# Two heads of the first k load moved from the casting DMA queue to an uncast one, with the casts on VectorE and ScalarE

## The chip, the cores and the metric

The kernel runs on one core of a Trainium2 chip. The metric is the device time of one launch in microseconds, the median of several runs. A core has TensorE (PE in the profile; its weight loads are listed as PEld), VectorE (DVE), ScalarE (ACT), GpSimd (POOL) and SyncE (SP). Three engines issue DMAs here: SyncE, ScalarE and GpSimd, each through a queue of its own, and the transfers of all queues run on the core's 16 DMA engines. In this kernel only GpSimd's loads change the type (f32 in memory, f16 in the tile); the loads that SyncE and ScalarE issue keep it.

## The reference

An attention with projected keys and values (batch 8, 8 heads, 1024 positions, head size 64, projection to 64), followed by a two-way maxout layer (8192 tokens, 512 to 1024 to 512):

```python
k_proj = einsum('ks,bhsd->bhkd', E, k)          # E, F: 64 x 1024
v_proj = einsum('ks,bhsd->bhkd', F, v)
scores = (q @ k_proj.T) / sqrt(64)
attn = softmax(scores)                           # over the 64 projected keys
x = (attn @ v_proj) transposed to (8192, 512)
out = maximum(x @ w1, x @ w2) @ w_out            # f32, 8192 x 512
```

All inputs and the output are f32 in memory; inside, the kernel multiplies in f16 and accumulates in f32.

## The kernel before, in words

The order of all work is written out by hand: the program order of each engine is the order in which the Python code emits its instructions, and the framework only adds the waits. There are three parts. The start (to about 30 us) handles batch 0's attention and loads everything. Then come sixteen units, two for each batch, each an up product and a down product (L691, L783; both by a seven-product scheme with sums made on VectorE), with the attention of the next batch's groups woven in at named slots. At the end the last unit's results are stored.

The change lies in the start. In program order it does this:

- **E and F** (64 x 1024 f32 each, 256 KB) are loaded into `ef_sb`, E by SyncE's queue (L77) and F by ScalarE's queue (L78). ScalarE then loads its function table (L79).
- **GpSimd's queue** carries all casting loads, in this order: k heads 0 to 3 of batch 0 (then the identity matrix is made on GpSimd), q heads 0 to 3, k heads 4 to 7, q heads 4 to 7, four loads of two heads of v, fourteen pieces of w1 and w2, w_out (`wo_sb`, L133), and from L938 on batch 1's k, v, q and batch 2's k. A load of four heads is 512 KB in f16. GpSimd issues each load of the weights only when a load eight places earlier has landed.
- **TensorE** first runs eight filler matmuls on a tile of ones (`warm`, L143), then eight transposes of E (L157), two fillers, eight transposes of F (L157), two fillers, and then the projection of k heads 0 to 3 (`step_kv`, L185, eight matmuls). Then follow two fillers, transposes of the projected k (L275), two fillers, transposes of q (L301), scores (L330) and so on.
- **VectorE** fills the ones tile (L136), casts the identity (L149), and copies E's transposes out of PSUM into `eft[0]` (L164). **ScalarE** copies F's transposes into `eft[1]` (L164). The projection of k needs `eft[0]`, that of v `eft[1]`.

The tiles that the change touches: `tiles[0]["k"]` (f16, 128 partitions x 8 heads x 8 x 64; a partition holds eight consecutive positions of each head), and `wo_sb` (f16, 128 x 8 x 512, 8 KB in each partition), which is used only after it is loaded at L133, with its sums (L542) at about 39 us.

Of the kernel before, what the change touches and what calls it, by code (L numbers as in the profile page):

```python
# [8 lines left out]
FP32 = mybir.dt.float32  # L9
FP16 = mybir.dt.float16  # L10
# [6 lines left out]
def kernel(  # L17
# [12 lines left out]
    nc = tc.nc  # L30

    B, H, S, D = q.shape
    KP = E.shape[0]
    DM = moe_w1.shape[0]
    DF = moe_w1.shape[1]
    NC = S // 128
    NI = NC // 2
    NFB = DF // 128
# [6 lines left out]
    const = ctx.enter_context(tc.tile_pool(name="const", bufs=1))  # L45
# [27 lines left out]
    def big(n, dtype=FP16):  # L73
        return const.tile([128, 16384 // mybir.dt.size(dtype) // 2], dtype, tag=f"big{n}", name=f"big{n}")

    ef_sb = big(0, FP32)[0:KP, :].rearrange("k (i s) -> k i s", i=2)
    nc.sync.dma_start(out=ef_sb[:, 0, :], in_=E)  # L77
    nc.scalar.dma_start(out=ef_sb[:, 1, :], in_=F)  # L78
    nc.scalar.add_instruction(  # L79
        mybir.InstLoadActFuncSet(  # L80
            name=nc.get_next_instruction_name(),
# [15 lines left out]
    def load(t, n, src, b, h0, h1):  # L97
        nc.gpsimd.dma_start(
            out=t[n][:, h0:h1],
            in_=src[b, h0:h1].rearrange("h (p c) d -> p h c d", c=NC),  # L100
        )

    tiles = {b: {} for b in range(B)}
    for n in ("k", "q", "v"):
        alloc(tiles[0], n)
    for h0 in (0, H // 2):
        for n, src in (("k", k), ("q", q)):
            load(tiles[0], n, src, 0, h0, h0 + H // 2)
            if (h0, n) == (0, "k"):
                ident = const.tile([128, 128], FP32)  # L110
                make_identity(nc, ident)
# [2 lines left out]

    w1_sb = big(1).rearrange("p (r f) -> p r f", r=NDC)
    w2_sb = big(2).rearrange("p (r f) -> p r f", r=NDC)
    wo_sb = const.tile([128, NFB, DM], FP16)
    for g in range(2):
        for w_sb, w in ((w2_sb, moe_w2), (w1_sb, moe_w1)):
            nc.gpsimd.dma_start(  # L120
                out=w_sb.rearrange("p (g z) f -> p g z f", z=2)[:, g, :, 0:256],
                in_=w.rearrange("(g p z) f -> p g z f", p=128, z=2)[:, g, :, 0:256],
            )
    for w_sb, w, f0, f1 in (
# [3 lines left out]
        for z in range(2):  # L128
            nc.gpsimd.dma_start(
                out=w_sb.rearrange("p (g z) f -> p g z f", z=2)[:, :, z, f0:f1],  # L130
                in_=w.rearrange("(g p z) f -> p g z f", p=128, z=2)[:, :, z, f0:f1],
# [15 lines left out]
    warm(8)  # L147
    ident16 = const.tile([128, 128], FP16)
    nc.vector.tensor_copy(out=ident16, in_=ident)  # L149


    eft = [const.tile([128, NC, KP], FP16, tag=f"eft{i}", name=f"eft{i}") for i in range(2)]

    for i in range(2):
        eft_ps = mm_bank()
        for c in range(NC):
            nc.tensor.transpose(  # L157
                out=eft_ps[:, c * KP : (c + 1) * KP],
                in_=ef_sb[:, i].rearrange("k (p c) -> k c p", c=NC)[:, c, :],
# [890 lines left out]
    for b in range(3, B):  # L1050
        t = tiles[b]
        n = 2 * b - 3
# [13 lines left out]
    for i, (new, old) in enumerate(zip([*groups[1:], none], groups)):  # L1066
        n, h = divmod(i + 2, 2)
# [70 lines left out]
```

## Time and profile before

| | |
|---|---|
| time, median of 3 runs | 321.56 us (321.26 to 321.61) |
| profiled execution: span, first to last instruction | 320.8 us (its whole device time is not given by the page) |
| TensorE busy | 313.7 us, 98% of the span |
| VectorE, ScalarE, GpSimd busy | 75%, 64%, 13% |
| mean granted TensorE clock | 0.994 |
| GpSimd's queue | 28.31 MB, 56.3% of the 16 DMA engines' span |
| HBM | 57.15 MB read, 16.78 MB written |

How to read it: TensorE is busy nearly all the time, so the other engines' shares tell only how much room they have. The chain of work that ended last follows the last instruction back to what released each step; its pieces name an engine or a DMA and a line. An issue row names the engine whose queue issued a DMA (SPq, ACTq, POOLq), the size in KB as stored, and the time from the issue to the landing. In the rows by stretch of time, the columns are the length, the busy time and instruction count of PE, PEld, DVE, ACT and POOL, then the granted clock (1.00 is full speed), the mean busy share of the 16 DMA engines (above 1 where packets overlap) and the GB/s that they moved, counted as stored.

### The profile page before, as it was taken

Reading aid. Unit: us, or ns where it says so; the run is one execution under the profiler, and the core shown is the slowest. Engines: PE = TensorE matmul, PEld = TensorE weight load, DVE = VectorE, ACT = ScalarE, POOL = GpSimd, SP = SyncE. Lnnn points to the kernel's source line nnn. Section 1 sums busy time; section 2 is a strip of 40 time slices with the busy share of each in tenths; the row PEclk is TensorE's granted clock in tenths of the full one; section 3 lists DMA queues with packets and bytes.
Section 4 is the critical chain, followed back from the end, with each engine's and each line's share of the span. In section 5 each row is a group of like instructions: output and inputs, shape, how many; then the busy total and the mean of one; then the engine's idle time right before and its main releaser. Section 6 shows DMA issues by size and latency. Waiting matters only on the chain.

```text
span 320.8 us, 9165 instructions
## 1 busy us (share of the span) xinstructions
PE 313.7 (98%) x3918; PEld 253.3 (79%) x3918; DVE 239.5 (75%) x432; ACT 205.3 (64%) x371; POOL 40.6 (13%) x63
## 2 busy tenths in 40 slices
PE   8899999999999999999999999999999999999996
PEld 3464588788887888888887888788887888888885
DVE  1246789787969787796969696896969696969683
ACT  1186752777775777576776777477776777765541
POOL 8259102003000300012000400021000000000000
PEclk9799999999999999999999999999999999999999
DMA  7999999997988899899999999899979231303023
GB/s 134 204 200 187 199 206 202 207 193 120 204 155 149 168 194 245 220 190 165 222 228 200 169 203 244 204 169 159 227 153 218 53 101 35 100 33 101 33 101 130
DMA packets 76408, 53.14 MB, mean 166 GB/s; under 512 B 29520, under 2 KB 76240, under 8 KB 76368
## 3 DMA queue, kind: packets, MB, share of 16 engines
q0 software_dynamic: 30944, 28.31, 56.3%
q1 hardware_dynamic: 45056, 23.80, 31.3%
q8 instruction: 30, 0.49, 0.6%
q10 hardware_dynamic: 368, 0.46, 0.6%
q14 instruction: 10, 0.08, 0.1%
HBM read 57.15 MB, written 16.78 MB: 230 GB/s over the span
## 4 chain that ended last, share of the span: by engine, by line
PE 94%; DMA 3%; ACT 1%; DVE 1%; issue 0%; DVEq 0%; POOLq 0%
PE mm_ps L783 46%; PE mm_ps L691 27%; PE mm_ps L477 4%; PE mm_ps L185 4%; PE att_ps L342 3%; DMA k_sb<-in_k_dram 3%; PE mm_ps L330 2%; PE mm_ps L579 2%; PE att_ps L227 1%; PE mm_ps L143 1%; PE mm_ps L301 1%; ACT ex_sb L370 1%; PE att_ps L330 0%; DVE qt_sb L306 0%; ACT ld_sb L382 0%; PE att_ps L502 0%
## 5 line engine op out<-in xcount | busy, mean ns | idle before, releaser
L665 ACT COPY p_sb<-mm_ps 128x512 f32<-128x512 f32 x179 | 101.7, 592 | 49.4 <-PE mm_ps L691 27.3
L783 PEld LDWEIGHTS <-big 128*128 128x128 f16 x768 | 73.5, 98 | 11.8 <-issue 3.6
L783 PE MATMUL mm_ps<-T_sb,big 128*128 128x256 f16 x576 | 77.0, 273 | 0.0
L706 DVE TENSOR_TENSOR gt_sb<-mm_ps,p_sb 128x512 f16<-128x512 f32 x56 | 38.5, 688 | 43.4 <-PE mm_ps L691 43.0
L691 PE MATMUL mm_ps<-big,big 128*128 128x256 f16 x336 | 50.4, 273 | 0.0
L691 PEld LDWEIGHTS <-big 128*128 128x128 f16 x448 | 43.8, 98 | 5.1
L783 PE MATMUL mm_ps<-wo_sb,gt_sb 128*128 128x256 f16 x256 | 42.8, 273 | 0.0
L783 PEld LDWEIGHTS <-gt_sb 128*128 128x128 f16 x376 | 35.6, 98 | 7.0 <-issue 3.0
L423 ACT ACTIVATE ex_sb<-mm_ps 128x512 f16<-128x512 f32 x50 | 27.2, 596 | 18.1 <-PE mm_ps L330 12.8
L691 PEld LDWEIGHTS <-wd_sb 128*128 128x128 f16 x336 | 32.8, 98 | 4.1
L691 PE MATMUL mm_ps<-xt_sb,wd_sb 128*128 128x256 f16 x224 | 33.0, 272 | 0.0
L452 DVE TENSOR_TENSOR xt_sb<-att_ps,ld_sb 128x1024 f16<-128x1024 f32 x26 | 31.7, 1219 | 0.2
L783 PE MATMUL mm_ps<-m_sb,xt_sb 128*128 128x256 f16 x128 | 24.4, 273 | 0.0
L813 DVE TENSOR_TENSOR o_sb<-mm_ps,p_sb 128x512 f32<-128x512 f32 x32 | 21.9, 683 | 2.8 <-ACT p_sb L837 2.0
L293 POOL COPY junk<-qt_sb 1x1 f16<-1x1 f16 x6 | 1.5, 244 | 175.7 <-DMA qt_sb<-q_sb 175.7
L709 DVE TENSOR_SCALAR gt_sb<-gt_sb 128x512 f16<-128x512 f16 (+1 forms) x60 | 21.7, 362 | 2.1
L651 DVE TENSOR_TENSOR big<-gt_sb 128x1024 f16<-128x1024 f16 x32 | 21.8, 683 | 0.0
L783 PE MATMUL mm_ps<-wo_sb,big 128*128 128x256 f16 x128 | 21.5, 273 | 0.0
L752 ACT ACTIVATE gt_sb<-mm_ps 128x512 f16<-128x512 f32 x28 | 16.8, 601 | 5.7 <-PE mm_ps L691 5.7
L783 PE MATMUL mm_ps<-T_sb,gt_sb 128*128 128x256 f16 x120 | 20.3, 273 | 0.0
L783 PEld LDWEIGHTS <-xt_sb 128*128 128x128 f16 x188 | 18.4, 98 | 2.1
L706 DVE TENSOR_TENSOR gt_sb<-p_sb 128x512 f16<-128x512 f32 x28 | 19.1, 682 | 0.7 <-ACT p_sb L665 0.6
(110 smaller groups left out, 435.1 us busy)
## 6 DMA issues: line engine op xcount, KB each, us to landing
out_dram<-o_sb SPq DMA_DIRECT2D x62, 256.0 KB, 2.9
k_sb<-in_k_dram POOLq DMA_DIRECT2D x7, 1024.0 KB, 10.2
v_sb<-in_v_dram POOLq DMA_DIRECT2D x7, 1024.0 KB, 16.8
q_sb<-in_q_dram POOLq DMA_DIRECT2D x5, 1024.0 KB, 23.4
q_sb<-in_q_dram POOLq DMA_DIRECT2D x6, 512.0 KB, 14.8
big<-in_moe_w_dram POOLq DMA_DIRECT2D x12, 128.0 KB, 6.6
k_sb<-in_k_dram POOLq DMA_DIRECT2D x2, 512.0 KB, 9.5
v_sb<-in_v_dram POOLq DMA_DIRECT2D x4, 256.0 KB, 14.3
```

The source lines that it names most:

```text
L185: nc.tensor.matmul(out=kv_ps[r * KP : (r + 1) * KP, h * D : (h + nh) * D], lhsT=eft[i][:, c, :], rhs=t[w][:, h0 + h : h0 + h + nh, c, :], ...
L423: nc.scalar.activation(out=t["ex", g, j][:, e, :], in_=banks[e], func=ACTF.Exp, scale=scale)
L452: nc.vector.tensor_tensor(out=x_out(t, g, j).rearrange("q z o n -> q o z n"), in0=at_ps.rearrange("q o (z n) -> q o z n", z=2), in1=ld[:, ...
L477: nc.tensor.matmul(out=h_ps, lhsT=wd_sb[:, r, fb * 128 : (fb + 1) * 128], rhs=t["xt"][:, r, :, j * W : (j + 1) * W], start=(r == 0), stop= ...
L651: nc.vector.tensor_tensor(out=S(i), in0=S(0) if x is None else x, in1=y(), op=op)
L665: copy(out=x, in_=bank)
L691: nc.tensor.matmul(out=bank[:, m * W : (m + 1) * W], lhsT=w_[:, n_, (2 * d + m) * 128 : (2 * d + m + 1) * 128], rhs=a[:, n_, :], start=(n ...
L706: nc.vector.tensor_tensor(out=c_blk(j, c), in0=two(x), in1=two(y), op=ALU.add)
L709: nc.vector.tensor_scalar_max(ap, ap, 0.0)
L752: nc.scalar.activation(out=out, in_=in_, func=ACTF.Relu)
L783: nc.tensor.matmul(out=bank[i][:, 0:CH] if two_banks else bank[:, i * CH : (i + 1) * CH], lhsT=a(c)[:, i * 128 : (i + 1) * 128], rhs=w_(c) ...
L813: nc.vector.tensor_tensor(out=o_sb, in0=two(x), in1=two(y), op=ALU.add)
```

## The change

Heads 0 and 1 of batch 0's k are no longer part of the first casting load. SyncE's queue fetches them as f32 (512 KB) into a new view `kf_sb`, which lies in the memory that `wo_sb` takes later (both tiles have the tag `wo`). VectorE casts head 0 and ScalarE casts head 1 from there into the f16 tile; each cast stands behind the identity's cast in the emitted order, so on VectorE ahead of the copy into `eft[0]`, and on ScalarE ahead of the copy into `eft[1]`. GpSimd's first load now brings heads 2 and 3 only (256 KB in f16). E goes from SyncE's queue to ScalarE's, and F from ScalarE's to SyncE's, behind k. The first projection matmul of k now waits for GpSimd's load, for both casts and for `eft[0]`. The load of w_out now waits for the casts as well, as they read its memory. The order of instructions on TensorE is the same; VectorE and ScalarE have one instruction more each, SyncE one more DMA.

```diff
     ef_sb = big(0, FP32)[0:KP, :].rearrange("k (i s) -> k i s", i=2)
-    nc.sync.dma_start(out=ef_sb[:, 0, :], in_=E)
-    nc.scalar.dma_start(out=ef_sb[:, 1, :], in_=F)
+    kf_sb = const.tile([128, 2048], FP32, tag="wo", name="kf_sb")[:, 0 : 2 * NC * D].rearrange(
+        "p (h c d) -> p h c d", h=2, d=D
+    )
+    nc.scalar.dma_start(out=ef_sb[:, 0, :], in_=E)
+    nc.sync.dma_start(out=kf_sb, in_=k[0, 0:2].rearrange("h (p c) d -> p h c d", c=NC))
+    nc.sync.dma_start(out=ef_sb[:, 1, :], in_=F)
...
     for h0 in (0, H // 2):
         for n, src in (("k", k), ("q", q)):
-            load(tiles[0], n, src, 0, h0, h0 + H // 2)
+            load(tiles[0], n, src, 0, h0 + 2 * ((h0, n) == (0, "k")), h0 + H // 2)
...
-    wo_sb = const.tile([128, NFB, DM], FP16)
+    wo_sb = const.tile([128, NFB, DM], FP16, tag="wo", name="wo_sb")
...
     ident16 = const.tile([128, 128], FP16)
     nc.vector.tensor_copy(out=ident16, in_=ident)
+    nc.vector.tensor_copy(out=tiles[0]["k"][:, 0], in_=kf_sb[:, 0])
+    nc.scalar.copy(out=tiles[0]["k"][:, 1], in_=kf_sb[:, 1])
```

## The prediction

> **What bounds the kernel now.** I read the page first: engine shares, the 40 slices, the clock row.
>
> ```profile
> PE 313.7 (98%) x3918; PEld 253.3 (79%) x3918; DVE 239.5 (75%) x432; ACT 205.3 (64%) x371; POOL 40.6 (13%) x63
> ...
> PEclk9799999999999999999999999999999999999999
> DMA  7999999997988899899999999899979231303023
> ```
>
> TensorE is busy for 98% of the span, so an edit pays only where TensorE waits or runs slowly. There is one slow slice, the second (8.0 to 16.0 us), and the DMA engines are full from the start to about 240 us. Next the chain that ended last, its first 14 us.
>
> ```profile
> 1.24 8.09 DMA k_sb<-in_k_dram
> 9.33 0.14 issue
> 9.47 1.57 PE mm_ps L185 x8
> 11.04 0.97 PE mm_ps L143 x2
> 12.01 0.35 PE mm_ps L275 x6
> 12.36 0.97 PE mm_ps L143 x2
> 13.33 0.47 PE mm_ps L301 x8
> ```
>
> The chain opens with the first load of k (four heads, by GpSimd's queue), from 1.24 to 9.33. It is the only load that TensorE waits for in the whole trace. Third, the timeline, for the order on TensorE ahead of it:
>
> ```profile
> 4.99 1.14 PE L157 MATMUL mm_ps<-ident,big 64*128 64x64 f32 x8
> 6.74 1.09 PE L157 MATMUL mm_ps<-ident,big 64*128 64x64 f32 x8
> 7.77 0.60 PE L143 MATMUL mm_ps<-ones 128*128 128x512 f16 x2
> 9.47 1.57 PE L185 MATMUL mm_ps<-k_sb,eft 128*64 128x256 f16 x8 [1.10 <-DMA k_sb<-in_k_dram]
> ```
>
> E's transposes at 4.99, F's at 6.74, two fillers to 8.37, then 1.10 us of nothing. F stands ahead of k on TensorE: a late F delays k's matmuls however early k is. Fourth, half-microsecond stretches (the last three columns: granted clock, DMA share, GB/s):
>
> ```profile
> 3.50:4.00 0.50, 0.50 (x3) 0.15 (x2) 0.00 (x0) 0.00 (x0) 0.50 (x1) 1.00 0.95 197
> 9.50:10.00 0.50, 0.50 (x5) 0.46 (x6) 0.00 (x0) 0.00 (x0) 0.38 (x1) 0.80 1.24 207
> 10.00:10.50 0.50, 0.50 (x4) 0.42 (x3) 0.00 (x0) 0.00 (x0) 0.33 (x1) 0.50 1.20 197
> 13.00:13.50 0.50, 0.50 (x7) 0.38 (x6) 0.00 (x0) 0.00 (x0) 0.00 (x0) 0.78 1.23 205
> ```
>
> The clock falls to 0.50 at 9.8, just after the idle 1.10 us, and is back at 13.2. So the late k costs twice. Last, the DMA issues by stretch (KB each, us from issue to landing):
>
> ```profile
> big<-in_E_dram SPq DMA_DIRECT2D x1, 256.0 KB, 3.7
> big<-in_F_dram ACTq DMA_DIRECT2D x1, 256.0 KB, 4.9
> q_sb<-in_q_dram POOLq DMA_DIRECT2D x1, 512.0 KB, 9.2
> v_sb<-in_v_dram POOLq DMA_DIRECT2D x1, 1024.0 KB, 19.6
> ```
>
> E and F, both issued at 0.74, land at 4.44 and 5.64. The first q, issued at 2.67, lands at 11.87; batch 1's v, issued at 29.30, lands at 48.9, and its matmuls (L227) begin at 50.06. GpSimd's queue moves 512 KB of f16 in 2.5 us (11.87 less 9.33), about 205 GB/s, and does so without a pause to 69.7 us: what shifts it shifts every load until then.
>
> **The change, part by part.** Write s for how much earlier GpSimd's stream of loads runs.
>
> *k on GpSimd's queue halves.* 256 KB leave its head: 256 KB at 205 GB/s is 1.25 us. Its issue shortens from 0.89 to about 0.71 (the two-head v loads), which is hidden: its first packets move only at 4.4 us.
>
> *k uncast on SyncE's queue adds 512 KB of f32.* No load of this kind is in the trace. The fast bound is the last stores, 340 GB/s alone: 1.5 us of all DMA engines. The slow bound is E and F, 0.52 MB between 2.1 and 4.5, or 217 GB/s: 2.4 us. What falls on GpSimd's stream is the part not done before its packets begin at 4.4. Until then the DMA share is about 0.9, against 1.24 when full, so a quarter of 2.4 us, 0.65 us, is free. With 1.5 us of work 0.85 falls on the stream, and s = 1.25 - 0.85 = +0.4. Ends: +1.25 if all of it fits before 4.4, -0.25 if none does. I take +0.4, since the share is measured in the very stretch. So k's other two heads land at 8.93 and q at 11.47.
>
> Here a rule speaks against the change. The Trainium skill, page DMA: Bandwidth & Descriptors, section Rules for kernel authors, says that spreading DMAs over several issuing queues gives no bandwidth, since all run on the same 16 engines. Taken strictly, the stream would go to the end -0.25 and the time to about 321.7; the share of 0.9 before 4.4 us is the room that the rule doesn't count.
>
> *E on ScalarE's queue, F behind k.* F lands at 5.64 now. With 512 KB more in front, it lands at 2.1 + 1.05 MB at 340 GB/s + 0.9 (from last data to landing, as E shows) = 6.1 at best, and at 5.64 + 2.4 = 8.0 at the slow rate, 8.8 if GpSimd's packets take a third of the later stretch. I take 7.0, the middle of the first two. Its issue waits 0.58 us behind k's on SyncE, which is inside this. TensorE then transposes F at 7.0 instead of 6.74, and the fillers end at 8.65 (+1.09, +0.60, less overlap). E can land up to 0.7 late on the second queue (F's first packets come 0.7 after E's now, with equal issue times); it was 0.55 early, so at most 0.2 us of TensorE time that F's wait swallows.
>
> *Two casts.* VectorE's 128x512 f32 to f16 from SBUF lies between 0.23 (the 128x128 identity cast) and 0.69 (the 128x512 copy of E's transposes); ScalarE's is near 0.59. k lands on SyncE's queue between 3.7 (a store's 2.2 us, plus 256 KB at 340 GB/s, after 0.74) and 7.0 (where F is taken); say 6.0. Behind VectorE's cast waits the copy of E's transposes, 0.69 long, now at 6.16: it ends at about 7.4. Behind ScalarE's waits F's copy, at 8.1 anyway. Both are ready before the matmuls of k, so they cost nothing; if k landed after about 7.6, VectorE's cast and copy (1.4 us) would become the last thing that L185 waits for.
>
> *Cost nothing.* The load of w_out now waits also for the casts, which end 20 us before its issue at 27.23. SyncE's next instruction is at 66.85.
>
> *The sum.* k's matmuls start at 8.93 + 0.14 = 9.07, against 9.47: 0.40. TensorE's idle time before them falls from 1.10 to about 0.4, plus 0.2 before F. A gap of 0.81 us at 24 us leaves the clock at 1.00, the gap of 1.10 did not, so I take it that the clock holds. From L185 to L301 then takes 0.99 (its eight matmuls at 16.11) + 0.70 (from their end to L275, same place) + 0.24 + 0.54 = 2.47 instead of 3.86 (9.47 to 13.33): 1.39 more. L301 would start at 11.54; q, landed at 11.47, lets it start at 11.6: 13.33 - 11.6 = 1.7 gained. Then the supply limits: batch 1's v has 50.06 - 48.9 - 0.14 = 1.0 us of slack, and comes 0.4 earlier, so TensorE can be at most 1.4 ahead there. **That is the gain: 1.4 us.** What is late next is that v, and with 1.5 of slack the transposed q of batch 2 (landed at 73.3, used at 74.87). The profiled span of 320.8 becomes 319.4. The page gives no total for its execution; the median of 321.56 stands 0.76 above the span, which I leave as it is: 320.2.
>
> On the clock a rule and a row differ. The Trainium skill, page TensorE: Matmul & The Clock Gate, section Why this matters for your kernels, wants no idle gaps above about 3 us, so a gap of 1.1 us should not lower the clock; this trace shows that it did. Were the drop unconnected with the gap, only the 0.40 of k would be left, 321.2.
>
> **The rivals.**
> *The clock falls anyway* at 9.8 until 13.2. k's matmuls are three quarters done by then; the rest at half rate brings L301's end to about 13.45 against 13.79: 0.35 gained, 321.2. For it: 0.6 us of idle time remains, and a delayed E adds to it. Against: the gap of 0.81.
> *The stream gains nothing* (s = -0.25): k's other heads land at 9.58, the gap stays, the clock falls; 0.25 lost there, less what the slack takes up: 321.6 to 321.8. For it: twice the bytes for half of k; against: the free share before 4.4.
> *F comes too late* (the slower side). L185 starts 1.65 after F lands. It is even with before at 7.8, and 0.64 slower at 8.46; at the bound of 8.8 it starts at 10.45, 1.0 late with the clock no better: 322.5. For it: F stands behind 512 KB on its queue; against: the queue moved 340 GB/s in the last stores.
>
> **How the numbers follow.** Forecast 0.58 (its own range 319.3 to 320.9), clock falls anyway 0.16, stream gains nothing 0.11, F (or the cast, behind a late k) too late 0.15. A measurement of this kernel can't tell a change within 0.2% (0.64 us) from none: the first case is faster, the second and third are within, the last is slower. The best end is F at its 7.0 with s = 1.25: L185 at 8.7, 0.77 + 1.39 = 2.2 gained, 319.3. The worst is 322.5.
>
> **What would show it.** k_sb from SyncE landing near 6, F near 7, the k load on GpSimd's queue at 8.9 and q near 11.5; no clock of 0.50 after 9.8; L301 at 11.6; L227 near 48.7, with a wait for v of some tenths. It is wrong if F's transposes start after 7.8, if GpSimd's loads don't come earlier, or if the clock falls all the same.

## The result, and the profile after

| | before | after |
|---|---|---|
| median of 9 runs | 321.26 us (320.99 to 322.29) | 322.39 us (322.06 to 323.45) |
| ratio, 95% interval | | 1.0039 [1.0026, 1.0052] |
| profiled execution | 322.6 us, worked out below (span 320.8, clock 0.994) | 322.30 us (span 320.5, clock 0.995) |

The change makes the kernel slower by 1.1 us. The two profiled spans say the opposite (320.8 before, 320.5 after), and this is the first thing to clear up. The device time of an execution is 1.72 to 1.85 us above the span in every execution listed with a span, of whatever kernel. By that the execution of before shown above took about 322.6 us: more than any of the three runs listed with it (321.26 to 321.61). It was a rare execution. Of 73 executions of before with their spans listed, 62 have a span of 319.2 to 320.3 us and a clock of 0.998 or more; four have a clock of 0.993 to 0.995, as it has.

The page of the changed kernel: engine busy times, then the clock and DMA rows of the 40 slices.

```profile
PE 313.7 (98%) x3918; PEld 253.4 (79%) x3918; DVE 240.2 (75%) x433; ACT 205.7 (64%) x372; POOL 40.0 (12%) x63
...
PEclk9799999999999999999999999999999999999999
DMA  8999999999939899899999899989979231303024
```

TensorE is as busy as before, with the same slow second slice. Now the chain that ended last, its first 11 us (start, length, what):

```profile
0.75 5.06 DMA big<-in_E_dram
5.80 0.14 issue
5.94 1.06 PE mm_ps L163 x8
7.00 0.54 PE mm_ps L147 x2
7.54 1.02 PE mm_ps L163 x8
8.56 0.79 PE mm_ps L147 x2
9.36 1.85 PE mm_ps L191 x8
```

It no longer opens with k on GpSimd's queue. It opens with E, which the prediction allowed 0.2 us. The timeline shows the wait, and the two new casts (in brackets: idle time before, and what ended it):

```profile
4.59 0.52 DVE L154 CAST k_sb<-kf_sb 128x512 f16<-128x512 f32 x1 [1.68 <-DMA kf_sb<-in_k_dram]
...
4.59 0.62 ACT L155 CAST k_sb<-kf_sb 128x512 f16<-128x512 f32 x1 [1.98 <-DMA kf_sb<-in_k_dram]
...
5.94 1.06 PE L163 MATMUL mm_ps<-ident,big 64*128 64x64 f32 x8 [0.89 <-DMA big<-in_E_dram]
...
9.29 1.92 PE L191 MATMUL mm_ps<-k_sb,eft 128*64 128x256 f16 x8
...
12.79 1.06 PE L307 MATMUL mm_ps<-ident,q_sb 128*128 128x128 f16 x16
```

The casts are over at 5.2, far ahead of any need. k's matmuls start at 9.29 without a wait for k. But TensorE idled 0.89 us before E's transposes, and k's eight matmuls take 1.92 instead of about 1.06. The half-microsecond stretches say why (the third number from the end is the granted clock):

```profile
8.50:9.00 0.50, 0.50 (x3) 0.11 (x2) 0.00 (x0) 0.40 (x1) 0.30 (x1) 0.71 1.27 213
9.00:9.50 0.50, 0.50 (x2) 0.18 (x2) 0.00 (x0) 0.19 (x1) 0.00 (x0) 0.50 1.24 205
...
12.00:12.50 0.50, 0.50 (x10) 0.31 (x10) 0.05 (x1) 0.00 (x0) 0.00 (x0) 0.87 1.26 207
```

The clock falls to 0.50 at about 8.7 and is back at about 12.1, with no wait for k anywhere. The DMA issues (KB as stored, us from issue to landing):

```profile
q_sb<-in_q_dram POOLq DMA_DIRECT2D x1, 512.0 KB, 7.7
kf_sb<-in_k_dram SPq DMA_DIRECT2D x1, 512.0 KB, 3.8
...
big<-in_E_dram ACTq DMA_DIRECT2D x1, 256.0 KB, 5.1
k_sb<-in_k_dram POOLq DMA_DIRECT2D x1, 256.0 KB, 6.6
big<-in_F_dram SPq DMA_DIRECT2D x1, 256.0 KB, 6.0
```

With the issues at 0.74 (k), 0.75 (E), 1.24 (GpSimd's k), 1.25 (F) and 2.61 (q), k's two heads land at 4.5, E at 5.8, F at 7.25, the other two heads at 7.8 and q at 10.3. The queues' rows by stretch explain E. From 3.0 to 3.5 us:

```profile
q1 hardware_dynamic: 99, 0.20, 106.4%
```

From 3.5 to 4.0 us:

```profile
q10 hardware_dynamic: 29, 0.12, 104.2%
q1 hardware_dynamic: 28, 0.03, 21.3%
```

SyncE's queue (q1) has all the DMA engines' time until k is through, and E on ScalarE's queue (q10) has no packet before 3.5 us, although both were issued at the same moment.

### The profile page after: what moved, and what is told of

Same layout as the page of the kernel before. It is cut to its first block, busy times and chain, and to the rows that moved or that the text cites. A ratio compares the mean times of both kernels' runs of the same rounds, so it can differ in the third digit from the quotient of the medians.

```text
span 320.5 us, 9170 instructions
## 1 busy us (share of the span) xinstructions
PE 313.7 (98%) x3918; PEld 253.4 (79%) x3918; DVE 240.2 (75%) x433; ACT 205.7 (64%) x372; POOL 40.0 (12%) x63
## 4 chain that ended last, share of the span: by engine, by line
PE 95%; DMA 2%; ACT 1%; DVE 1%; issue 0%; DVEq 0%
PE mm_ps L789 46%; PE mm_ps L697 27%; PE mm_ps L483 4%; PE mm_ps L191 4%; PE att_ps L348 3%; PE mm_ps L336 2%; PE mm_ps L585 2%; DMA big<-in_E_dram 2%; PE mm_ps L147 1%; PE att_ps L233 1%; PE mm_ps L307 1%; PE mm_ps L163 1%; ACT ex_sb L376 1%; PE att_ps L336 0%; DVE qt_sb L312 0%; ACT ld_sb L388 0%
## 5 line engine op out<-in xcount | busy, mean ns | idle before, releaser
L429 ACT ACTIVATE ex_sb<-mm_ps 128x512 f16<-128x512 f32 x50 | 27.2, 597 | 18.0 <-PE mm_ps L336 12.8
```

Source lines behind the costliest of these rows:

```text
L429: nc.scalar.activation(out=t["ex", g, j][:, e, :], in_=banks[e], func=ACTF.Exp, scale=scale)
```

## The experiments

Each ratio is to the kernel before on the same chip in the same session. One piece of work has another line number in each kernel: E's and F's transposes are L163 in after and L157 in before, the projections L191 and L185 (L189 in e3), q's transposes L307 and L301, the first products with w L483 and L477.

**e1: only E and F change queues.** The kernel before with nothing else of the change.

```diff
-    nc.sync.dma_start(out=ef_sb[:, 0, :], in_=E)
-    nc.scalar.dma_start(out=ef_sb[:, 1, :], in_=F)
+    nc.scalar.dma_start(out=ef_sb[:, 0, :], in_=E)
+    nc.sync.dma_start(out=ef_sb[:, 1, :], in_=F)
```

> The kernel before with E on ScalarE's queue and F on SyncE's; no uncast k, no casts. Theory 'late E' (E's place on the second queue and beside the uncast k costs TensorE's first transposes): alone it lands E 0.7 us later at most (near 5.1), TensorE waits 0.1 to 0.3 us, hidden before k's landing at 9.33; span within 0.3 of 320.8, time as before. Theory 'outside' (the time that lies outside the traced span, 1.8 us in all nine runs after the change, has grown by about 1 us, through something that the change adds): if the swap does it, outside is 1.8 and the time is 1 us longer with an unchanged span; if not, outside is below 1.

Measured: 322.98 us, ratio 1.0054 [1.0041, 1.0067], where no loss was expected. The DMA issues, then the timeline of TensorE:

```profile
big<-in_F_dram SPq DMA_DIRECT2D x1, 256.0 KB, 3.6
big<-in_E_dram ACTq DMA_DIRECT2D x1, 256.0 KB, 4.8
```

```profile
5.71 1.07 PE L157 MATMUL mm_ps<-ident,big 64*128 64x64 f32 x8 [0.97 <-DMA big<-in_E_dram]
...
9.84 1.89 PE L185 MATMUL mm_ps<-k_sb,eft 128*64 128x256 f16 x8 [0.48 <-DMA k_sb<-in_k_dram]
```

E lands 4.8 us after its issue, at 5.55, TensorE idles 0.97 us, and the clock is at 0.50 from about 7.7 to 14.5 us. The profiled execution is the longest of the five (span 322.0, clock 0.989); the other four have spans of 321.1 to 321.5 at 0.998 or 0.999. The place of E alone costs at least about as much as the whole change, with no uncast k at all: behind F's 256 KB, E lands only 0.25 us earlier than behind k's 512 KB in after.

**e4: E first again, the rest of the change kept.** E goes back to the head of SyncE's queue, with k behind it there and F on ScalarE's.

```diff
-    nc.scalar.dma_start(out=ef_sb[:, 0, :], in_=E)
+    nc.sync.dma_start(out=ef_sb[:, 0, :], in_=E)
+    nc.scalar.dma_start(out=ef_sb[:, 1, :], in_=F)
     nc.sync.dma_start(out=kf_sb, in_=k[0, 0:2].rearrange("h (p c) d -> p h c d", c=NC))
-    nc.sync.dma_start(out=ef_sb[:, 1, :], in_=F)
```

> The changed kernel with E first on SyncE's queue, k behind it there, and F on ScalarE's queue as before. Theory 'late E': E lands near 4.5 and F near 6, TensorE doesn't wait for E, k's matmuls start between 8.0 and 8.6 instead of 9.29, and the span shrinks by 0.6 to 1.3 against the changed kernel (319.2 to 319.9). Theory 'outside': the outside part stays at 1.8, so the time is 321.0 to 321.7. If E's place isn't the cause the span stays at 320.5.

Measured: 321.20 us, ratio 0.9992 [0.9978, 1.0005]. The loss is gone: E lands at 4.4, TensorE does not wait for it, and ten of eleven spans are 319.1 to 319.8. But k's matmuls start at 9.15, later than the 8.0 to 8.6 expected. k now lands at 8.05, VectorE's cast stands in front of the copy of E's transposes, and that copy is the last thing k's matmuls wait for:

```profile
9.15 1.06 PE L191 MATMUL mm_ps<-k_sb,eft 128*64 128x256 f16 x8 [0.97 <-DVE eft L170]
```

This is the effect that the prediction described for a k landing after 7.6, and here it costs 0.97 us of waiting. The clock nevertheless stays at 1.00 behind that wait, so an idle stretch of nearly a microsecond does not always bring it down.

**e2: is something outside the span?** Two dead copies of the casts' shape, 128x512, are added to before (one on VectorE, one on ScalarE, into the memory of w_out); the ones tile and its fill move ahead of them. This tested an early theory of mine, that the casts or their code cost time outside the traced span, since the spans alone showed no loss.

```diff
...
+    dead = const.tile([128, NFB, DM], FP16, tag="wo", name="dead")
+    nc.vector.tensor_copy(out=dead[:, 0], in_=ones16)
+    nc.scalar.copy(out=dead[:, 1], in_=ones16)
...
```

> The kernel before with one more 128x512 copy on VectorE and one on ScalarE in the start, into w_out's memory, nothing else. Theory 'outside through the longer instruction streams': outside 1.8 instead of below 1, time about +1 us, span 320.8. Rival 'outside through the added load': outside below 1, time within 0.3 of before. The copies lie in idle time of both engines (before 2.7 us), so the span shouldn't move by more than 0.2.

Measured: 321.25 us, ratio 1.0005 [0.9982, 1.0029], and the time outside the span is 1.8 us as everywhere. That theory fell. A side finding mattered more: in this profile k lands 7.0 us after its issue, not 8.1, and TensorE does not wait for it. That made me doubt the execution that I had predicted from.

**e3: the uncast load alone.** Before, with the two heads of k also fetched uncast behind E on SyncE's queue and never used; GpSimd's loads stay whole.

```diff
...
+    nc.sync.dma_start(out=kf_sb, in_=k[0, 0:2].rearrange("h (p c) d -> p h c d", c=NC))
...
```

> The kernel before with the uncast load of two heads of k added on SyncE's queue behind E, into w_out's memory and read by nobody; E, F and GpSimd's loads as before. It moves 512 KB more. Theory 'outside through the added load': outside 1.8, time +1 us beyond what the span shows. Rival: outside below 1. In the span, k from GpSimd's queue lands about 0.8 later (10.1), so the span grows by about 0.8 to 321.6.

Measured: 322.59 us, ratio 1.0038 [1.0026, 1.0051]. TensorE's timeline:

```profile
9.52 1.88 PE L189 MATMUL mm_ps<-k_sb,eft 128*64 128x256 f16 x8 [1.33 <-DMA k_sb<-in_k_dram]
```

The added load delays GpSimd's k, TensorE waits 1.33 us, and the clock is at 0.50 from 9.2 to 12.5. The queue rows from 5.5 to 6.0 us show it:

```profile
q1 hardware_dynamic: 93, 0.19, 103.4%
```

GpSimd's packets (q0) come in number only from about 6.0, when the uncast loads are nearly through. They did so at about 4.7 in before and 5.5 in after.

**e5: before, profiled again.** The same kernel as before, profiled a second time.

> The kernel before, unchanged, profiled once more. Theory 'rare execution': the trace that the prediction was read from, with a span of 320.8 and a clock of 0.994, is not what the kernel usually does; 18 of 21 later executions have a span of 319.4 to 319.9 and a clock of 0.999 or 1.000. Then k lands near 8.2 to 8.4 instead of 9.33, TensorE waits for no load, the clock stays at 1.00 after the first filler matmuls, and the span is 319.4 to 319.9. Rival: the same trace as before, with k at 9.3 and the clock at 0.50 from 9.8.

Measured: 321.40 us, span 319.6, clock 1.00, so one of the usual executions. Timelines of TensorE and VectorE:

```profile
8.29 1.03 PE L185 MATMUL mm_ps<-k_sb,eft 128*64 128x256 f16 x8
...
10.81 1.07 PE L301 MATMUL mm_ps<-ident,q_sb 128*128 128x128 f16 x16
...
19.53 0.64 PE L185 MATMUL mm_ps<-v_sb,eft 128*64 128x128 f16 x16 [0.62 <-DMA v_sb<-in_v_dram]
...
23.30 0.43 DVE L493 TENSOR_TENSOR wd_sb<-big,big 128x512 f16<-128x512 f16 x1 [0.16 <-DMA big<-in_moe_w_dram]
...
23.78 1.90 PE L477 MATMUL mm_ps<-xt_sb,wd_sb 128*128 128x512 f16 x8
```

TensorE does not wait for k at all: E lands at 4.7, ahead of its transposes at 4.98, k lands at about 8.2, its matmuls start at 8.29, and the clock holds. What is waited for instead is v at 19.53 and a piece of w at 23.3, both later loads of GpSimd's stream. So the two terms that made most of my forecast were not there to be gained.

**e6: k on ScalarE's queue, E at the head of SyncE's.** My theory after e1 and e4 was that E comes late because ScalarE's queue starts late.

```diff
-    nc.scalar.dma_start(out=ef_sb[:, 0, :], in_=E)
-    nc.sync.dma_start(out=kf_sb, in_=k[0, 0:2].rearrange("h (p c) d -> p h c d", c=NC))
+    nc.sync.dma_start(out=ef_sb[:, 0, :], in_=E)
+    nc.scalar.dma_start(out=kf_sb, in_=k[0, 0:2].rearrange("h (p c) d -> p h c d", c=NC))
     nc.sync.dma_start(out=ef_sb[:, 1, :], in_=F)
```

> The changed kernel with E and then F on SyncE's queue and the uncast k alone on ScalarE's. Theory 'late E' (E on ScalarE's queue lands 1.4 us late and costs TensorE the wait and the clock): E lands near 4.5, F near 5.7, no wait before the transposes, k's matmuls at 8.3 to 8.6, no clock of 0.50, time 320.9 to 321.4, so same as before or up to 0.5 us better, since GpSimd's stream then runs up to 0.5 earlier. Rival 'the uncast k itself costs' (DMA engines taken from E and F): time 322 or more.

Measured: 323.43 us, ratio 1.0065 [1.0049, 1.0080]; the theory fell. The DMA issues, then TensorE's timeline:

```profile
kf_sb<-in_k_dram ACTq DMA_DIRECT2D x1, 512.0 KB, 4.4
...
big<-in_E_dram SPq DMA_DIRECT2D x1, 256.0 KB, 5.7
```

```profile
6.60 1.06 PE L163 MATMUL mm_ps<-ident,big 64*128 64x64 f32 x8 [1.54 <-DMA big<-in_E_dram]
8.76 1.15 PE L163 MATMUL mm_ps<-ident,big 64*128 64x64 f32 x8 [0.56 <-DMA big<-in_F_dram]
```

E is on SyncE's queue, at its head, and still lands last of the two, at 6.4, because k on the other queue goes first (197 packets of k and none of E between 2.5 and 3.5 us). So ScalarE's queue as such is not what makes E late, and the rival's 322 or more came true for this order; e4 shows that the uncast k costs nothing where E goes ahead of it. k's issue takes 0.45 us, E's 0.58, so k's ends first, at 1.19 against 1.32. In the changed kernel it is the same (0.46 for k, 0.55 for E). Where the lengths are about equal (0.58, in before and e1), SyncE's went first. The load whose packets start first holds the DMA engines until it is nearly done. What lets it start first is not settled: k had the shorter issue each time, so the end of the issue and the kind of load can't be told apart here. Nor does k's being first explain all of E's delay in e6: k's packets are nearly over by 4.0 us, and then, from 4.5 to 5.5, the DMA engines move only 49 GB/s, for a reason that the trace does not show.

**e8, e9: the changed kernel again**, for a second and a third profile.

> The changed kernel, profiled once more: its executions come in two kinds, spans of 320.3 to 320.6 with a mean clock of 0.995, and 321.1 to 321.7 with 0.998 or 0.999. The first kind is the trace at hand. Should the second show: theory 'TensorE starts slow and stays slow for longer', the first 10 to 12 us of matmuls run at half rate (0.43 us for a filler of 512 columns) without a fall of the clock in the records. Rival: the clock is full and k or F lands 0.6 to 1.2 us later than in the first kind.

> The changed kernel unchanged, timed beside the next three. Theory 'clock': two executions of it, equal to 8.5 us, differ only in that the clock falls at 8.71 in one (span 320.5) and not in the other (318.9). So the executions should fall into groups: span near 318.9 with a clock of 1.000, near 320.5 with 0.995, and 321 to 322 with 0.998 or 0.999; the mean depends on how many fall into each. Rival 'this chip is faster for it': all near 318.9.

Measured: e8 320.71 us (span 318.9, one run); e9 322.55 us, ratio 1.0023 [1.0002, 1.0044] on a chip where before itself had nine of 35 executions above a span of 320.5. TensorE's timeline in e8:

```profile
1.46 3.60 PE L147 MATMUL mm_ps<-ones 128*128 128x512 f16 x8 [1.46 <-DVE ones L140]
...
5.93 1.07 PE L163 MATMUL mm_ps<-ident,big 64*128 64x64 f32 x8 [0.88 <-DMA big<-in_E_dram]
...
9.03 1.06 PE L191 MATMUL mm_ps<-k_sb,eft 128*64 128x256 f16 x8
...
11.29 1.06 PE L307 MATMUL mm_ps<-ident,q_sb 128*128 128x128 f16 x16
...
23.42 1.90 PE L483 MATMUL mm_ps<-xt_sb,wd_sb 128*128 128x512 f16 x8
```

TensorE's timeline in e9's profiled execution (span 321.6):

```profile
6.00 1.12 PE L163 MATMUL mm_ps<-ident,big 64*128 64x64 f32 x8 [0.95 <-DMA big<-in_E_dram]
...
9.10 1.04 PE L147 MATMUL mm_ps<-ones 128*128 128x512 f16 x2
10.06 1.92 PE L191 MATMUL mm_ps<-k_sb,eft 128*64 128x256 f16 x8
...
13.97 1.06 PE L307 MATMUL mm_ps<-ident,q_sb 128*128 128x128 f16 x16
```

Three executions of one kernel, alike until about 5.9 us, and apart afterwards by TensorE's speed alone: in e8 the clock holds, in the first profile it falls at 8.7 (L307 at 12.79), and in e9 TensorE works at half rate until about 13.5 (two fillers in 1.04 instead of 0.60, k's matmuls in 1.92). The last kind the clock column does not show. In e9 it gives 1.00 from the first filler on:

```profile
9.00:9.50 0.50, 0.50 (x4) 0.13 (x2) 0.00 (x0) 0.30 (x1) 0.00 (x0) 1.00 1.25 209
```

The column misses half rate at the start of every trace here, too: the first eight fillers take 3.6 us, 0.45 each (3.27 in e1; in e11 five take 2.31), with a clock of 1.00 recorded, as in the prediction's row from 3.50 to 4.00. TensorE starts slow in all of them; what differs is whether it is fast once E's transposes begin, and whether it stays so.

Of the 22 executions of the changed kernel with spans listed (nine with the result, e8, twelve of e9), two have a span of 318.9 with the clock held, ten 320.2 to 320.6 at a clock of 0.993 to 0.995, and ten 321.1 to 321.8 at 0.998 to 1.00. One execution of each group was profiled (e8, the first profile and e9), and that the others of a group went the same way is taken from their spans and clocks.

**e7, e10: cover for E's wait.** Ten, then twelve fillers ahead of E's transposes instead of eight, the change otherwise as it is.

```diff
-    warm(8)
+    warm(12)
```

> The changed kernel with ten filler matmuls instead of eight ahead of E's transposes, so that TensorE stays busy until E lands. E stays late. If the clock that falls is most of the loss: no clock of 0.50 near 8.7 to 12.1, q's transposes (L307) at about 11.6 instead of 12.8, span 319.4 to 319.8, time near 321.4. If the delay of the chain by 0.9 us is the loss, span and time stay within 0.3 of the changed kernel (320.5, 322.4).

> The changed kernel with twelve fillers ahead of E's transposes instead of eight. Theory 'clock': TensorE no longer idles for E, so the clock falls in fewer executions than with ten fillers (2 to 4 of 12); most spans near 319.0 to 319.4, the median 320.7 to 321.1, under that of the kernel before (321.4). Rival: the late transposes alone cost it, span 320 or more throughout; or the extra fillers push the transposes back by up to 0.6 and the spans by as much.

Measured: with ten, 320.85 us, ratio 0.9992 [0.9976, 1.0008]; with twelve, 321.08 us, ratio 0.9977 [0.9956, 0.9999]. With ten 0.44 us of idle time is left in the profiled execution, whose clock falls (span 320.5); eight of the twelve executions have spans of 318.9 to 319.3. With twelve none is left:

```profile
1.46 4.96 PE L147 MATMUL mm_ps<-ones 128*128 128x512 f16 x12 [1.46 <-DVE ones L140]
...
6.35 1.09 PE L163 MATMUL mm_ps<-ident,big 64*128 64x64 f32 x8
...
9.47 1.06 PE L191 MATMUL mm_ps<-k_sb,eft 128*64 128x256 f16 x8
```

Though the transposes start 0.4 later than in the changed kernel, eleven of twelve spans lie between 318.9 and 320.2. This version is faster than the changed kernel by 1.5 us in the same session (322.55 against 321.08). Than before it is 0.4 us faster by the medians, but the interval only just leaves out 1, and before had nine of its 35 executions above a span of 320.5 in that session, against none of 17 and two of 21 in the other two. The four fillers do two things at once: they cover the wait, and they keep TensorE at work for longer before E's transposes. Which of the two keeps it fast, these runs do not separate; e4, which takes the wait away without a filler more, also ends the loss.

**e11: the idle time without the load.** Before with five fillers instead of eight, so that TensorE idles before an E that lands when it always did.

```diff
-    warm(8)
+    warm(5)
```

> The kernel before with five fillers ahead of E's transposes instead of eight, no other edit: TensorE idles from about 3.7 to E's landing at 4.5 to 4.8, as long as it idles for E after the change, while every load comes as before. Theory 'clock': many executions with a span of 320.3 to 322 and a clock of 0.989 to 0.999, median 322 or more. Rival 'late loads are the loss, the idle time by itself is harmless': spans of 319.3 to 319.9 as before, time 321.1 to 321.6.

Measured: 321.75 us, ratio 1.0007 [0.9992, 1.0022]. TensorE's timeline in the profiled execution (span 321.0):

```profile
4.38 1.11 PE L157 MATMUL mm_ps<-ident,big 64*128 64x64 f32 x8 [0.61 <-DMA big<-in_E_dram]
...
8.89 1.89 PE L185 MATMUL mm_ps<-k_sb,eft 128*64 128x256 f16 x8 [0.39 <-DMA k_sb<-in_k_dram]
```

TensorE is at half rate in this one, with a clock of 1.00 recorded. Over eleven executions the median span is 320.0 against 319.7 for before, so the median of 322 or more did not come, and 0.6 us of idle time (with fewer fillers ahead of it) does less harm than the 0.9 us in after. Nine of the eleven spans are 319.4 to 320.2. It doesn't settle how much of the harm the idle time does.

**e12: one head instead of two.** The changed kernel with 256 KB of uncast k, one cast, and three heads in GpSimd's first load.

```diff
-    nc.sync.dma_start(out=kf_sb, in_=k[0, 0:2].rearrange("h (p c) d -> p h c d", c=NC))
+    nc.sync.dma_start(out=kf_sb, in_=k[0, 0:1].rearrange("h (p c) d -> p h c d", c=NC))
...
-    nc.scalar.copy(out=tiles[0]["k"][:, 1], in_=kf_sb[:, 1])
```

> The changed kernel with one uncast head of k instead of two (256 KB on SyncE's queue ahead of F; GpSimd's first load brings three heads; one cast, on VectorE). Theory 'E waits for the uncast k': E lands near 5.1 instead of 5.8, TensorE idles 0.1 to 0.3 us instead of 0.9, and fewer executions lose the clock; spans 319.0 to 319.5, median 320.8 to 321.4. Rival: E's place on the second queue alone makes it late (5.5 to 5.8, as with the swap alone), then 322 or more.

Measured: 321.46 us, ratio 0.9995 [0.9977, 1.0014]. TensorE's timeline in the profiled execution (span 321.3):

```profile
5.15 1.11 PE L162 MATMUL mm_ps<-ident,big 64*128 64x64 f32 x8
...
9.20 1.92 PE L190 MATMUL mm_ps<-k_sb,eft 128*64 128x256 f16 x8
```

E lands at 5.05, as the fillers end, and ten of twelve spans are 318.5 to 320.2. The other two are 321.3; one of them is the profiled one, at half rate until about 13.5 with no idle stretch of note. So half rate can come without an idle stretch, here in one profiled execution and, by its span, perhaps in one more of the twelve.

## Why the prediction was wrong

I forecast 320.2 us, faster; the time is 322.39, slower than before. That it lies inside my range is luck: the upper end, 322.5, came from a late F, and F was not late.

*The base.* The sum started from an execution that was itself one of before's rare ones, and I added the 0.76 us by which the median exceeded its span. The runs show 1.8 us outside the span, so that execution was at 322.6. The page gave me the span alone, but e5 shows what the usual execution looks like: k lands 6.9 us after its issue and not 8.1, TensorE doesn't wait for it, and the clock holds. The step "k's matmuls start at 9.07 against 9.47: 0.40" and the step "2.47 instead of 3.86: 1.39 more" removed losses that, by their spans and clocks, 62 of 73 executions don't have.

*E "at most 0.2 us of TensorE time".* This is the step that turned the sign. It measured 0.89 us. I costed E's place as the 0.7 us between the first packets of E and F in the trace I read. But a load is of use only when it has landed, and in that same trace F, on the second queue, landed 1.2 us after E (5.64 against 4.44). e1 shows this cost alone: with no uncast k, E behind F lands at 5.55 and TensorE idles 0.97 us. With k's 512 KB in front, E has no packet before 3.5 us and lands at 5.8, 1.4 us later than in the trace I read (4.44) and 1.1 later than in the usual execution (4.7), not 0.7.

*"I take it that the clock holds."* By span and clock, TensorE lost its full rate in 20 of 22 executions; profiled are one fall of the clock and one run at half rate. I had weighed k's gap of about 0.4 and 0.2 before F against a stretch of 0.81 us at 24 us that left the clock up. The stretch that came was 0.89 us, before f32 transposes and in the first microseconds. From the start of k's matmuls to q's transposes the changed kernel then takes 3.50 us (9.29 to 12.79) against 2.26 when the clock holds (e8), and the span goes from 318.9 to 320.5 or more. The Trainium skill, page TensorE: Matmul & The Clock Gate, section Why this matters for your kernels, has gaps above about 3 us as the danger. Here a stretch of 0.89 us went ahead of the fall in the first profile, as 1.10 us did in the trace of before, while e8 kept the clock after the same stretch: in this kernel a gap far below 3 us is not safe, though it does not always bring the fall. My rival "the clock falls anyway" named this mechanism, but with 0.16 and at 321.2, from the same wrong base.

*The stream, s = +0.4.* Right, by the usual execution: GpSimd's two heads land at 7.84 against 8.18, q at 10.3 against 10.8, so 0.35 to 0.45 earlier. The landings I gave (8.93 and 11.47) were a microsecond too late, because the trace I read had them late. The gain is there and is seen when the clock holds: e8 has no wait for v, its first L483 matmuls start at 23.42 against 23.78, TensorE is 0.63 us ahead by 27.2 us (27.16 against 27.79 for the same matmuls), and the span is 318.9 against 319.6. So the change is worth 0.7 us, not 1.4, in the two executions of 22 that keep the clock, and the way is through v and w in batch 0's later loads, not through k and the clock. The rule on spreading DMAs over queues (the Trainium skill, page DMA: Bandwidth & Descriptors, section Rules for kernel authors) would have given nothing here; GpSimd's loads landed earlier all the same. It is no clean test of the rule, as the change also swaps casting packets for uncast ones and uses time before 4.4 us in which the DMA engines were not full. The lower end of s was too mild by its own terms: -0.25 takes the fast rate, and the slow one with the same free room gives 1.25 - (2.4 - 0.65) = -0.5.

*k on SyncE's queue, "say 6.0".* It landed at 4.5: 0.19 to 0.20 MB in each half microsecond between 2.5 and 3.5, about 390 GB/s, above my fast bound of 340.

*F "7.0", and the rival of a late F.* F landed at 7.25, and its transposes start at 7.47 straight behind the fillers, which E's delay had already pushed back: TensorE did not wait for F. k's matmuls start at 9.29, as the next two fillers end. The cause of the slower side was E, although it stood at the head of its queue.

*The casts.* 0.52 us on VectorE and 0.62 on ScalarE, both at 4.59 and hidden. The bounds were 0.23 to 0.69 and near 0.59. Right.

The account in measured spans: 319.6 (before, e5) less 0.7 (the stream, e8) plus 1.6 (the fallen clock, 320.5 against 318.9) gives 320.5, with 1.8 outside the span 322.3; the median is 322.39. These terms are differences of the spans themselves, so they must add up; what supports the split is that 1.50 of the 1.6 us is there by q's transposes (12.79 in the first profile against 11.29 in e8). The executions at 321.1 to 321.8 cost 2.2 to 2.9 over 318.9. With E's wait covered by four fillers (e10), or E put ahead of k (e4), the loss goes.

What stays open is what exactly decides the clock. An idle stretch of 0.97 us that ended at 9.15 left it up (e4), one of 0.88 that ended at 5.9 did in e8 and not in most others, and e12 was at half rate once without one. That E's wait makes it likely is shown: spans of 320.2 or more have 20 of 22 executions of after and 5 of 5 of e1, against 1 of 11 in e4, 2 of 12 with twelve fillers and 14 of 73 of before. The rule behind it is not.

## What to carry to other kernels

Before reading waits and gaps out of a profile, check that the profiled execution is a usual one: its total against the listed runs. A wait that only a rare execution has is not there to be gained. When a load that an engine waits for at the start comes second to another, price its delay by when the other is through, from landings and not from first packets, and look at what the engine's clock does with the idle stretch, which can cost more than the stretch does.

## What the runs showed of the hardware

- Of two uncast loads issued together on two queues, one gets nearly all of the DMA engines until it is nearly through: 190 packets of k to none of E between 2.5 and 3.5 us in after. k went first on either queue, and E's landing followed k's by 1.3 us in after (5.8 and 4.5), in e6 (6.4 and 5.1) and in e12 (5.05 and 3.7). Whether k's shorter issue (0.39 to 0.46 us against 0.55 to 0.58) or its kind decides is not shown.
- GpSimd's casting loads get few packets until the uncast ones are through: they came in number at about 4.7 us in before, 5.5 in after and 6.0 in e3 and e4.
- TensorE starts at half rate in every trace here (eight 512-column fillers in 3.6 us), and can stay or be there until about 13.5 us (e9: two fillers in 1.04 us, in e8 in 0.60), both with a recorded clock of 1.00. The lengths of instructions show it, the clock column does not.
- Time outside the span was 1.72 to 1.85 us in all executions, whatever was added to the kernel.
